# Two gated FFT-convolution layers and two MLPs, forward and backward, on one core: a reordered opening, other changes of order, and the product of the convolved k with v on GpSimd

## The chip, the cores and the metric

The kernel runs on one core of a Trainium2 chip. Its engines are named as in the profile: PE is TensorE (matrix products and transposes into PSUM), DVE is VectorE, ACT is ScalarE, POOL is GpSimd, and SP is the engine that issues most DMAs. Each engine runs its own instructions in a fixed order, and they wait for each other by semaphores. The time of a run is its device time in microseconds (us). All times below are in us unless they are marked ns.

## The reference, cut to what matters

```python
def _A_ref(q, k, v, shift_k, ssm_k, ssm_D):
    k_shift = sum over t < 4 of k_pad[:, t:t + S, :] * shift_k[:, 3 - t]
    kv = k_shift * v
    y = irfft(rfft(kv, 2 * S) * rfft(ssm_k, 2 * S))[:S]
    y = y + kv * ssm_D
    return q * y

def _B_ref(x, w1, w2):
    return silu(x @ w1) @ w2

x = A_q
x = x + _A_ref(layernorm(x), A_k, A_v, A_shift_k, A_ssm_k, A_ssm_D)
x = x + _B_ref(layernorm(x), B_w1, B_w2)
x = x + _A_ref(layernorm(x), A_k, A_v, A_shift_k, A_ssm_k, A_ssm_D)
x = x + _B_ref(layernorm(x), B_w1, B_w2)
```

S is 2048, the width D is 448 and the inner width F is 1792; the data are bf16. Both layers share their weights, and so the convolution result y is the same in both. What is computed is x and the gradients with respect to eight inputs, for a given grad_out: nine outputs.

## The kernel before

The work is done in three parts.

**The opening, `_ssm_prefix`,** makes y. The FFT of 4096 points is split in two stages, each of them matrix products on PE. `_fft_stage1` takes ssm_k over the long axis into A1K. `turn` (L348) transposes sixteen 128x128 blocks of it, group g of seven, into Z. `_fft_stage2` takes chunks of 1024 columns (14 of them, NCI) through the small DFT, and the function it is given gets the result from PSUM: `cons_ka` copies it to Ka (the memory of Z), stores every second chunk pair to DRAM (spec_K, L400), and for the later chunks issues the two DMAs of `_swap_halves_dma` (L244 and L245), which write KB, Ka with its halves swapped. On the side of the data, `conv(h, jq)` does the short convolution of k on PE for one of eight pieces (two column halves h, four row groups jq); ACT copies its result to ks (L372), POOL issues the store of ks to DRAM (KS_d, L374), and DVE multiplies ks by v to kvt (L376). `stage1_kv` takes kvt through stage 1 (L386) one loop step later, into A1kv; it is then turned into Zkv, and stage 2 over Zkv hands each chunk to `cons_prod`: a copy to Zf (the memory of A1K), a store (spec_KV, L443), and the products pa = Zf * Ka (L449) and pb = Zf * KB (L450) on DVE. Two chunks later `_fft_inv_stage2_chunk` takes pa and pb back (L226, L227), and the last stage (L475) makes Ysb, which is y. `_Bal` keeps a running sum of planned load for ACT and DVE, and gives each PSUM copy to the engine that has less; `_copy` shows as L111 on ACT and L113 on DVE.

In program order the opening runs: a loop over h = 0 and 1 and the four jq, which does conv, stage1_kv of the piece before, and then for h = 0 two turns of A1K, for h = 1 two chunks of K's stage 2; then the swaps of the first four chunk pairs, the last stage1_kv, K's remaining chunks 8 to 13, the LayerNorm of the first rows, all seven turns of A1kv, and stage 2 of kv with its products.

**`Main.run`** goes over four chunks c of 512 rows. `H(c, L)` (L is the layer) multiplies by w1: seven tiles fp of two blocks of 128 rows of F, each into a PSUM tile ps_h with two buffers (tag "mm", which ps_g shares). Of every tile ACT makes aT by silu (L614), and a copy of the tile goes to dT, on DVE where fp is in the argument dv and on ACT elsewhere. `slope` later replaces dT by silu's derivative on ACT (L626). `O` multiplies aT by w2 (L633) and adds to X. `G` makes the gradient behind w2 (ps_g, L652), whose PSUM copy ghT is multiplied by dT on DVE (L668 and L800). `N` multiplies by w1 (L683) and goes through the LayerNorm's backward `_ln_bwd`. `T` and `T2` are transposes on PE (L525, L723), copied by ACT to nT. `_ln` is a forward LayerNorm (bn_stats is L259, the power rstd on POOL L266, the normalised n L273), `fwd0` and `fwd1` are the two of them that stand ahead of a layer, with the gate by Y. PE's order is written out by `weave`, whose letters take one step from each generator; the order of DVE, ACT and POOL is chosen by the framework's scheduler when the kernel is built, within what `issue_after(x)` (put in behind x) and `keep_in_program_order` demand.

**`Jobs`** makes the weight gradients (L924): groups of four products (a unit), taken from a generator wherever PE is to have work of this kind. `bank` says which PSUM buffer a group sums in: "mm" has two, "tr" one, which the transposes use. **`_ssm_suffix`** takes the gradient back through the FFTs, with `jobs.run(n)` between its steps: a first stage (L206), `spectrum` (L1132, two parts u for each of seven pairs cp), the inverse (L1145), `ps_gkv` (L1189, eight steps i, copied by ACT to gkv, L1191), and the gradients of ssm_k and shift_k, for which four copies make skmask (L1218). What is left of the jobs runs at the end.

## Time and profile before

| what | us |
|---|---|
| runs of the kernel, median of 3 (lowest, highest) | 750.91 (748.93, 752.5) |
| the profiled execution, its own time | 744.07 |
| its span in the trace | 742.3 |
| granted clock, mean | 0.997 |

The busy time of the engines by stage of the profiled execution (the stages are cut by TensorE's instructions):

| from | to | stage | PE | DVE | ACT | POOL |
|---|---|---|---|---|---|---|
| 0 | 25.37 | loads, FFT stage 1 of ssm_k, transposes of k | 19.30 | 13.22 | 15.01 | 3.60 |
| 25.37 | 102.22 | the rest of the opening | 67.68 | 65.53 | 61.57 | 24.06 |
| 102.22 | 172.20 | first G, H(0,0), O, fwd1, G, H(0,1), O | 63.31 | 41.99 | 47.99 | 10.50 |
| 172.20 | 477.80 | the loop over the chunks | 300.22 | 198.95 | 216.23 | 23.69 |
| 477.80 | 519.66 | the last chunk's backward, with jobs | 40.63 | 18.52 | 10.24 | 2.71 |
| 519.66 | 691.00 | the backward FFTs, with jobs | 164.91 | 120.73 | 93.03 | 52.21 |
| 691.00 | 742.30 | the last gradients and jobs | 44.98 | 24.29 | 5.18 | 9.97 |

A stage's length less PE's busy time is what PE waited there: 9.2 in the opening's second row, 6.7 in the third, 5.4 in the long fourth. Rows of the timeline give the start, the duration, the engine, the line, and at the end in brackets how long the engine had been idle and what released it. Durations of neighbouring instructions overlap, since they are pipelined: the distance of two starts is what one costs.

### The profile page before, as it was taken

How to read it: one execution, taken by the hardware profiler on the slowest of the kernel's cores; microseconds unless marked ns; L12 is line 12 of the kernel's file. 1: busy time of each engine (PE TensorE's matmuls, PEld its weight loads, DVE VectorE, ACT ScalarE, POOL GpSimd, SP SyncE). 2: the span in 40 equal slices, each digit the busy share in tenths (PEclk: the TensorE clock that was granted, in tenths of full speed). 3: DMA queues.
4: the chain of work that ended last, by engine and by line, in shares of the span. 5: the costliest groups of instructions: out<-in, count | busy, mean ns of one | idle time of the engine just before them, and what ended most of it. 6: DMA issues, size and time to landing. Idle time of an engine off the chain costs nothing.

```text
span 742.3 us, 12705 instructions
## 1 busy us (share of the span) xinstructions
PE 701.0 (94%) x4947; PEld 395.2 (53%) x4976; DVE 483.2 (65%) x1140; ACT 449.3 (61%) x572; POOL 126.7 (17%) x212
## 2 busy tenths in 40 slices
PE   6998888989999999999999999999989999989996
PEld 4876644435444444444444544545466666657553
DVE  4789855856686747856379523925158769879760
ACT  4887966688866968669677794132755555455100
POOL 1134410210011100201001100000221234244130
PEclk9999999999999999999999999999999999999999
DMA  9949699799979999589875998189997898789870
GB/s 324 271 148 289 234 281 176 139 233 229 231 181 228 236 239 210 101 211 256 190 183 118 246 228 312 27 191 236 348 411 263 266 331 297 230 304 353 294 226 19
DMA packets 195485, 172.40 MB, mean 232 GB/s; under 512 B 142850, under 2 KB 173698, under 8 KB 194272
## 3 DMA queue, kind: packets, MB, share of 16 engines
q1 hardware_dynamic: 180896, 115.53, 61.7%
q0 software_dynamic: 14064, 56.04, 22.0%
q8 instruction: 39, 0.64, 0.4%
q14 instruction: 22, 0.18, 0.1%
q10 hardware_dynamic: 464, 0.00, 0.0%
HBM read 73.06 MB, written 60.10 MB: 179 GB/s over the span
## 4 chain that ended last, share of the span: by engine, by line
PE 41%; issue 21%; ACT 7%; DMA 7%; DVE 6%; POOL 3%; POOLq 0%; ACTq 0%; DVEq 0%
PE ps_d L924 11%; PE ps_h L611 9%; PE ps_n L683 6%; PE ps_o L633 5%; PE ps_g L652 3%; ACT dT L626 3%; DMA out_dram<-dout 2%; PE ps_v L227 2%; PE ps_v L226 2%; DMA go<-in_grad_out_dram 1%; DVE ln_st L259 1%; ACT aT L614 1%; POOL rstd L266 1%; DMA Minvs<-c_minv 1%; ACT dT L111 1%
## 5 line engine op out<-in xcount | busy, mean ns | idle before, releaser
L611 PE MATMUL ps_h<-nT,w1sb 112*128 112x512 bf16 x448 | 104.4, 379 | 6.9 <-ACT dT L111 2.9
L924 PEld LDWEIGHTS <-dstat 128*128 128x128 bf16 x800 | 75.7, 98 | 64.5 <-issue 0.6
L683 PE MATMUL ps_n<-w1T,ghT 128*128 128x448 bf16 x448 | 95.3, 353 | 1.3 <-DVE ghT L668 1.2
L633 PE MATMUL ps_o<-w2sb,aT 128*128 128x448 bf16 x448 | 88.5, 352 | 0.0
L652 PE MATMUL ps_g<-nT,w2T 128*128 128x512 bf16 x378 | 86.6, 379 | 0.7
L666 ACT CAST ghT<-ps_g 128x1024 bf16<-128x1024 f32 (+1 forms) x67 | 53.5, 821 | 53.0 <-PE ps_g L652 53.0
L614 ACT ACTIVATE aT<-ps_h 128x1024 bf16<-128x1024 f32 (+1 forms) x72 | 58.4, 834 | 34.9 <-PE ps_h L611 32.1
L611 PEld LDWEIGHTS <-w1sb 112*128 112x128 bf16 x448 | 43.8, 98 | 59.7 <-issue 10.2
L652 PEld LDWEIGHTS <-w2T 128*128 128x128 bf16 x448 | 43.7, 98 | 51.7 <-issue 0.7
L849 DVE SCALAR_TENSOR_TENSOR lb_v<-lb_u,n 128x448 bf16<-128x448 bf16 x48 | 29.9, 623 | 63.0 <-ACT lb_u L687 62.6
L683 PEld LDWEIGHTS <-ghT 128*128 128x128 bf16 x448 | 43.2, 98 | 43.9 <-DVE ghT L668 3.6
L633 PEld LDWEIGHTS <-aT 128*128 128x128 bf16 x448 | 43.5, 98 | 40.1
L626 ACT ACTIVATE dT<-dT 128x1024 bf16<-128x1024 bf16 (+1 forms) x64 | 54.6, 936 | 0.1
L266 POOL TENSOR_TENSOR rstd<-ln_ve,mhalf 128x2 f32<-128x2 f32 (+2 forms) x27 | 22.3, 827 | 178.2 <-DVE ln_ve L264 178.2
L924 PE MATMUL ps_d<-n3m,dstat 128*128 128x448 bf16 x224 | 48.2, 352 | 0.2
L924 PE MATMUL ps_d<-n1m,dstat 128*128 128x448 bf16 x224 | 48.1, 352 | 0.2
L111 ACT CAST dT<-ps_h 128x1024 bf16<-128x1024 f32 (+1 forms) x54 | 48.0, 906 | 0.0
L226 PE MATMUL ps_v<-Gsb,pa 128*128 128x128 bf16 x336 | 43.8, 222 | 2.7 <-DVE pa L449 2.6
L227 PE MATMUL ps_v<-Gsb,pb 128*128 128x128 bf16 x336 | 42.9, 222 | 2.4 <-DVE pb L450 1.9
L687 ACT ACTIVATE lb_u<-ps_n,rstd 128x448 bf16<-128x448 f32 x32 | 20.7, 646 | 31.8 <-PE ps_n L683 18.1
L924 PE MATMUL ps_d<-go,dstat 128*128 128x448 bf16 x176 | 37.2, 352 | 0.4 <-DMA go<-in_grad_out_dram 0.4
L226 PEld LDWEIGHTS <-pa 128*128 128x128 bf16 x336 | 33.3, 99 | 7.9 <-DVE pa L449 4.7
(208 smaller groups left out, 1193.0 us busy)
## 6 DMA issues: line engine op xcount, KB each, us to landing
dstat<-g_d SPq DMA_DIRECT2D x28, 512.0 KB, 6.0
dstat<-a_d SPq DMA_DIRECT2D x26, 512.0 KB, 5.8
a_d<-turned SPq DMA_DIRECT2D x16, 512.0 KB, 3.7
g_d<-turned SPq DMA_DIRECT2D x16, 512.0 KB, 3.5
a_d<-turned SPq DMA_DIRECT2D x16, 384.0 KB, 2.9
g_d<-turned SPq DMA_DIRECT2D x16, 384.0 KB, 2.9
N_d<-n POOLq DMA_DIRECT2D x10, 448.0 KB, 5.4
spec_K<-Z POOLq DMA_DIRECT2D x7, 512.0 KB, 6.6
```

The costliest lines, as they stand in the source:

```text
L111: nc.scalar.copy(out, in_)
L226: nc.tensor.matmul(pv[:, i, :], lhsT=pa[:, i * P:(i + 1) * P], rhs=k.Gsb[:, ga, :], start=True, stop=False)
L227: nc.tensor.matmul(pv[:, i, :], lhsT=pb[:, i * P:(i + 1) * P], rhs=k.Gsb[:, gb, :], start=False, stop=True)
L611: nc.tensor.matmul(ps[:, u, :], lhsT=self.w1sb[:, dc, ft * P:(ft + 1) * P], rhs=nT[:DC, dc, :], start=(dc == 0), stop=(dc == ND - 1))
L614: self.last_silu = nc.scalar.activation(aT[hh][:, o:o + hi - lo, :], ps[:, lo:hi, :], ACT.Silu)
L626: self.nc.scalar.activation(d[:, o:o + n, :], d[:, o:o + n, :], ACT.Derivative_silu)
L633: nc.tensor.matmul(po[:, :D], lhsT=aT[ft // 7][:, ft % 7, tl * P:(tl + 1) * P], rhs=self.w2sb[:, ft, :], start=(ft == 0), stop=(ft == NF - 1))
L652: nc.tensor.matmul(ps[:, u, :], lhsT=self.w2T[:, b, ft * P:(ft + 1) * P], rhs=gT[:, b, :], start=(b == 0), stop=(b == ND - 1))
L666: nc.scalar.copy(g, ps[:, lo:hi, :])
L683: nc.tensor.matmul(pn[:, :D], lhsT=gh[ft // 7][:, ft % 7, tl * P:(tl + 1) * P], rhs=self.w1T[:, ft, :], start=(ft == 0), stop=(ft == NF - 1))
L849: nc.vector.scalar_tensor_tensor(out=v[:], in0=u0, scalar=-1.0 / D, in1=n_t, op0=ALU.mult, op1=ALU.mult, accum_out=cp[:, 1:2])
L924: self.nc.tensor.matmul(ps[:, :D], lhsT=st[:, t, :], rhs=mov[:, t, :], start=(first and t == 0), stop=(last and t == NT - 1))
```

## The change

1. **`_ln` gets `behind`:** its bn_stats are put in behind a given DVE instruction. For `fwd0` of c >= 1 that is the last product dT * ghT of the last G (`self.g_last`), for `fwd1(c + 1)` the last instruction of `_ln_bwd` (`self.chain`, which `_ln_bwd` now returns).
2. **kvt** (ks times v, 128x896, eight times) is computed by POOL in place of DVE, and the balance counts nothing for it.
3. **stage1_kv** copies both halves of its PSUM tile in one instruction (16 in place of 32).
4. **The opening's order:** in the h = 1 half, K's stage 2 runs chunks 0-3, 4-7, 8-10 and 11-13, and three turns of A1kv (g = 0, then 1 and 2) are done there. The swaps of all seven pairs are issued behind the loop. Then come the last stage1_kv, chunks 0 to 5 of kv's stage 2, the LayerNorm, turns 3 to 6 with the products of chunks 0 to 5 between them, and chunks 6 to 13 with a product after each. The copy and store of a chunk (`cons_x`) are separated from its products (`prod`).
5. **x0c0 and gb0** are loaded by SP, behind the transposing load of w2T, and not by POOL.
6. **H:** where a tile's copy is on DVE, its silu and its copy are split in halves. H(0, 1) copies all seven tiles on DVE (before: tiles 3 and 5); the H of later chunks copy tile 5 on DVE where c is 0 or L is 1 (before: none).
7. **`slope(dT1)`** issues its last two small pieces behind the last copy of the transposes to nT (`self.last_copy`).
8. **Jobs and the suffix:** group 4 sums in the bank "tr", no longer in "mm"; two more units run in the first `spectrum`, and four more between the first four `ps_gkv` steps; skmask is copied by POOL.

```diff
@@ -249,14 +249,17 @@
-def _ln(k, pool, c, src, si, n_g, groups=((0, 4),), pin=False, eng=None):
+def _ln(k, pool, c, src, si, n_g, groups=((0, 4),), pin=False, eng=None, behind=None):
     nc = k.nc
...
         for tl in range(lo, hi):
-            i = nc.vector.bn_stats(out=st[:, tl, :], in_=src(tl))
+            with ExitStack() as es:
+                if behind is not None:
+                    es.enter_context(k.tc.issue_after(behind.ins))
+                i = nc.vector.bn_stats(out=st[:, tl, :], in_=src(tl))
             if pin:
@@ -321,7 +324,7 @@
         nc.sync.dma_start_transpose(out=k.w2T[:, 0:3, :], in_=k.B_w2[:, 0:384])
-        nc.sync.dma_start_transpose(out=k.w2T[:, 3:4, :], in_=k.B_w2[:, 320:448])
+        w2 = nc.sync.dma_start_transpose(out=k.w2T[:, 3:4, :], in_=k.B_w2[:, 320:448])
@@ -373,8 +376,7 @@
             kvt = work.tile([P, 4, DH], BF16, name="kvt", tag="pb", bufs=3)
-            nc.vector.tensor_tensor(out=kvt[:], in0=ks[:], in1=vn[:, 4 * jq:4 * jq + 4, ds], op=ALU.mult)
-            bal.add("dve", 0.62)
+            nc.gpsimd.tensor_tensor(out=kvt[:], in0=ks[:], in1=vn[:, 4 * jq:4 * jq + 4, ds], op=ALU.mult)
             return kvt
@@ -384,9 +386,8 @@
                         nc.tensor.matmul(ps[:, w, c, :DH], lhsT=k.M1sb[:, n2 + w, c, :], rhs=kvt[:, u + w, :], start=True, stop=True)
-                for w in range(2):
-                    _copy(nc, bal.pick(2 * DH), A1kv[:, 56 * h:56 * (h + 1), :, n2 + w, :].rearrange("p dh c ds -> p c dh ds"),
-                          ps[:, w, :, :DH].rearrange("p c (dh ds) -> p c dh ds", ds=4))
+                _copy(nc, bal.pick(4 * DH), A1kv[:, 56 * h:56 * (h + 1), :, n2:n2 + 2, :].rearrange("p dh c n ds -> p c dh n ds"),
+                      ps[:, :, :, :DH].rearrange("p n c (dh ds) -> p c dh n ds", ds=4))
@@ -395,10 +396,41 @@
                 lo, hi = (ci - 1) * 1024, (ci + 1) * 1024
-                if ci > 8:
-                    _swap_halves_dma(k, KB, Ka, lo, hi, nc.gpsimd)
                 nc.gpsimd.dma_start(out=k.SPEC_d["K"][:, lo:hi], in_=Ka[:, lo:hi])
+        B1 = A1kv[:].rearrange("p a c n s -> p a (c n s)")
+        Zf = A1K[:].rearrange("p a c n s -> p (a c n s)")
+
+        def cons_x(ci, ps):
+            sl = slice(ci * 1024, (ci + 1) * 1024)
+            _copy(nc, bal.pick(1024), Zf[:, sl], ps[:])
+            if ci % 2 == 1:
+                st = nc.gpsimd.dma_start(out=k.SPEC_d["KV"][:, (ci - 1) * 1024:(ci + 1) * 1024], in_=Zf[:, (ci - 1) * 1024:(ci + 1) * 1024])
+            if ci == 3:
+                with tc.issue_after(st.ins):
+                    nc.gpsimd.memset(k.w2T[0:64, 3, :], 0.0)
+
+        hold = []
+
+        def prod(ci):
+            sl = slice(ci * 1024, (ci + 1) * 1024)
+            pa = work.tile([P, 1024], BF16, name="pa", tag="pa", bufs=4)
+            pb = work.tile([P, 1024], BF16, name="pb", tag="pb", bufs=3)
+            nc.vector.tensor_tensor(out=pa[:], in0=Zf[:, sl], in1=Ka[:, sl], op=ALU.mult)
+            nc.vector.tensor_tensor(out=pb[:], in0=Zf[:, sl], in1=KB[:, sl], op=ALU.mult)
+            bal.add("dve", 1.4)
+            hold.append((pa, pb, ci))
+            if len(hold) > 2:
+                pa, pb, cj = hold.pop(0)
+                _fft_inv_stage2_chunk(k, pa, pb, False, B1, cj, psum)
+
+        k.x0c0 = _hd(k, [P, 4, D], "x0c0")
+        k.gb0 = _hd(k, [P, 4, D], "gb0")
+        with tc.issue_after(w2.ins):
+            nc.sync.dma_start(out=k.x0c0[:], in_=_pm(k.A_q[0])[:, 0:4, :])
+            nc.sync.dma_start(out=k.gb0[:], in_=_pm(k.grad_out[0])[:, 0:4, :])
+
+        spans = ((0, 4), (4, 8), (8, 11), (11, 14))
         prev = None
@@ -411,50 +443,28 @@
                 else:
-                    _fft_stage2(k, Z, psum, cons_ka, range(2 * i, 2 * i + 2))
-        for i in range(4):
+                    _fft_stage2(k, Z, psum, cons_ka, range(*spans[i]))
+                    for g in ((), (), (0,), (1, 2))[i]:
+                        turn(B1, Zkv, g)
+        for i in range(7):
             _swap_halves_dma(k, KB, Ka, 2048 * i, 2048 * (i + 1), nc.gpsimd)
         stage1_kv(*prev)
-        _fft_stage2(k, Z, psum, cons_ka, range(8, NCI))
+        _fft_stage2(k, Zkv, psum, cons_x, range(6))
...
         nc.sync.dma_start(out=k.w1sb[:], in_=k.B_w1.rearrange("(c p) f -> p c f", p=DC))
-        k.gb0 = _hd(k, [P, 4, D], "gb0")
-        nc.gpsimd.dma_start(out=k.gb0[:], in_=_pm(k.grad_out[0])[:, 0:4, :])
-        k.x0c0 = _hd(k, [P, 4, D], "x0c0")
-        nc.gpsimd.dma_start(out=k.x0c0[:], in_=_pm(k.A_q[0])[:, 0:4, :])
         k.na0 = _hd(k, [P, 4, D], "na0")
...
-        B1 = A1kv[:].rearrange("p a c n s -> p a (c n s)")
-        Zf = A1K[:].rearrange("p a c n s -> p (a c n s)")
-
-        A1f = A1kv[:].rearrange("p a c n s -> p a (c n s)")
-        for g in range(7):
-            turn(A1f, Zkv, g)
-        hold = []
-
-        def cons_prod(ci, ps):
...
-        _fft_stage2(k, Zkv, psum, cons_prod)
+        for g in range(3, 7):
+            turn(B1, Zkv, g)
+            if g < 6:
+                prod(2 * (g - 3))
+                prod(2 * (g - 3) + 1)
+        for ci in range(6, NCI):
+            _fft_stage2(k, Zkv, psum, cons_x, (ci,))
+            prod(ci)
@@ -586,15 +596,15 @@
             src = lambda tl: xc[:, tl, :]
-            self.a_fwd(c, 0, src, n00, ((0, 4),))
+            self.a_fwd(c, 0, src, n00, ((0, 4),), self.g_last)
         n01 = self.t([P, 4, D], "n01", bufs=2)
...
-    def fwd1(self, c):
+    def fwd1(self, c, behind=None):
         n10, n11 = self.t([P, 4, D], "n10"), self.t([P, 4, D], "n11")
         pairs = ((0, 2), (2, 4)) if c else ((0, 2), (2, 3), (3, 4))
-        self.a_fwd(c, 2, self.xs(c), n10, pairs)
+        self.a_fwd(c, 2, self.xs(c), n10, pairs, behind)
         _ln(self.k, self.ch, c, self.xs(c), 3, n11, pairs)
@@ -609,18 +619,18 @@
                     nc.tensor.matmul(ps[:, u, :], lhsT=self.w1sb[:, dc, ft * P:(ft + 1) * P], rhs=nT[:DC, dc, :], start=(dc == 0), stop=(dc == ND - 1))
-            for lo, hi in self.parts(fp):
+            for lo, hi in ((0, 1), (1, 2)) if fp in dv else self.parts(fp):
                 hh, o = divmod(2 * fp + lo, 7)
                 self.last_silu = nc.scalar.activation(aT[hh][:, o:o + hi - lo, :], ps[:, lo:hi, :], ACT.Silu)
-            for lo, hi in ((0, 2),) if fp < 6 else ((0, 1), (1, 2)):
+            for lo, hi in ((0, 2),) if fp < 6 and fp not in dv else ((0, 1), (1, 2)):
                 _copy(nc, nc.vector if fp in dv else nc.scalar, self.dpart(dT, 2 * fp + lo, 2 * fp + hi), ps[:, lo:hi, :])
...
     def slope(self, dT, behind=None):
-        with self.tc.issue_after((behind or self.last_silu).ins):
-            for d in dT:
+        for i, d in enumerate(dT):
+            with self.tc.issue_after((behind if behind is not None and i > 2 else self.last_silu).ins):
                 n = min(2, d.shape[1])
@@ -665,7 +675,7 @@
                 if dT is not None:
-                    nc.vector.tensor_tensor(out=g, in0=d, in1=g, op=ALU.mult)
+                    self.g_last = nc.vector.tensor_tensor(out=g, in0=d, in1=g, op=ALU.mult)
             yield
@@ -690,7 +700,7 @@
                 nc.vector.scalar_tensor_tensor(out=u1[:], in0=Gt, scalar=k.rstd[2][:, t:t + 1], in1=self.Y[:, t, :], op0=ALU.mult, op1=ALU.mult, accum_out=cp[:, 4 + tl, 0:1])
-                _ln_bwd(k, self.ch, u1[:], n_a[:, tl, :], cp[:, 4 + tl, :], Gt, Gt)
+                self.chain = _ln_bwd(k, self.ch, u1[:], n_a[:, tl, :], cp[:, 4 + tl, :], Gt, Gt)
             else:
@@ -771,7 +782,7 @@
         r = []
-        weave("H" * 7, H=self.H(0, 1, nT, r, (3, 5)))
+        weave("H" * 7, H=self.H(0, 1, nT, r, range(7)))
         for c in range(4):
@@ -810,13 +821,13 @@
                 if c == 0:
-                    weave("NTNTNHNHNHNHNHHHH", N=n, T=self.T(self.n0[1][1], nT, NBLK), H=self.H(c + 1, 0, nT, r))
+                    weave("NTNTNHNHNHNHNHHHH", N=n, T=self.T(self.n0[1][1], nT, NBLK), H=self.H(c + 1, 0, nT, r, (5,)))
                 else:
...
                 weave("OOOOOOTOTO", O=self.O(c + 1, 0, aT), T=tg)
-                self.fwd1(c + 1)
+                self.fwd1(c + 1, self.chain)
                 g = self.G(gT, gh1, dT0)
@@ -824,7 +835,7 @@
                     weave("G" * 7, G=g)
-                self.slope(dT1)
+                self.slope(dT1, self.last_copy)
             else:
@@ -837,7 +848,7 @@
                 nT = self.nT()
-                weave("NNTNTNHNHNHNHNHHH", N=n, T=self.T(self.n1[1], nT, NBLK), H=self.H(c + 1, 1, nT, r))
+                weave("NNTNTNHNHNHNHNHHH", N=n, T=self.T(self.n1[1], nT, NBLK), H=self.H(c + 1, 1, nT, r, (5,)))
             else:
@@ -851,7 +862,7 @@
     nc.vector.tensor_tensor(out=v[:], in0=v[:], in1=u0, op=ALU.add)
-    nc.vector.tensor_tensor(out=G_out, in0=v[:], in1=g_res, op=ALU.add)
+    return nc.vector.tensor_tensor(out=G_out, in0=v[:], in1=g_res, op=ALU.add)
@@ -928,7 +939,7 @@
             self.n_bank += 1
-        bufs = {"po": 2, "jb": 1, "mm": 2}[tag]
+        bufs = {"po": 2, "jb": 1, "mm": 2, "tr": 1}[tag]
         if tag == "mm":
@@ -971,7 +982,7 @@
         yield from self.group((3,), keys, (go, g2), self.fin_w2, tags=("jb",))
-        yield from self.group((4,), keys, (go, g2), self.fin_w2, tags=("mm",))
+        yield from self.group((4,), keys, (go, g2), self.fin_w2, tags=("tr",))
         yield from self.group((5, 6), keys, (go, g2), self.fin_w2)
@@ -1131,7 +1142,7 @@
                     nc.scalar.copy(Zf[cp][:, u * 1024:(u + 1) * 1024], ps[:])
-                    jobs.run(1)
+                    jobs.run(1 if cp else 2)
                 _swap_halves(k, xsw, Zf[cp])
@@ -1192,7 +1203,7 @@
             nc.vector.tensor_tensor(out=gks[:, sl, :], in0=gkv, in1=gks[:, sl, :], op=ALU.mult)
-            jobs.run(1)
+            jobs.run(2 if i < 4 else 1)
         for lo, hi in ((0, 112), (112, 127)):
@@ -1215,7 +1226,7 @@
         for b in range(0, P, 32):
-            nc.vector.tensor_copy(mask[b:b + 32, :], k.ident[b:b + 32, b:b + 32])
+            nc.gpsimd.tensor_copy(mask[b:b + 32, :], k.ident[b:b + 32, b:b + 32])
         pd = psum.tile([P, 2, 512], FP32, name="ps_sk", **mm)
```

More of the change, by code (lines that the diff above doesn't have):

```diff
@@ L431, in _ssm_prefix @@
-        Zf = A1K[:].rearrange("p a c n s -> p (a c n s)")
-        A1f = A1kv[:].rearrange("p a c n s -> p a (c n s)")
-        for g in range(7):
-            turn(A1f, Zkv, g)
-        hold = []
-        def cons_prod(ci, ps):
-            sl = slice(ci * 1024, (ci + 1) * 1024)
-            xs = Zf[:, sl]
-            _copy(nc, bal.pick(1024), xs, ps[:])
-            if ci % 2 == 1:
-                st = nc.gpsimd.dma_start(out=k.SPEC_d["KV"][:, (ci - 1) * 1024:(ci + 1) * 1024], in_=Zf[:, (ci - 1) * 1024:(ci + 1) * 1024])
-            if ci == 3:
-                with tc.issue_after(st.ins):
-                    nc.gpsimd.memset(k.w2T[0:64, 3, :], 0.0)
-            pa = work.tile([P, 1024], BF16, name="pa", tag="pa", bufs=4)
-            pb = work.tile([P, 1024], BF16, name="pb", tag="pb", bufs=3)
-            nc.vector.tensor_tensor(out=pa[:], in0=xs, in1=Ka[:, sl], op=ALU.mult)
-            nc.vector.tensor_tensor(out=pb[:], in0=xs, in1=KB[:, sl], op=ALU.mult)
-            bal.add("dve", 1.4)
-            hold.append((pa, pb, ci))
-            if len(hold) > 2:
-                pa, pb, cj = hold.pop(0)
-                _fft_inv_stage2_chunk(k, pa, pb, False, B1, cj, psum)
@@ L547, in parts, with a_fwd @@
         return [(0, 2)] if fp not in (3, 6) else [(0, 1), (1, 2)]
-    def a_fwd(self, c, si, src, n_g, groups):
+    def a_fwd(self, c, si, src, n_g, groups, behind=None):
         nc, X = self.nc, self.X
@@ L556, in a_fwd @@
             return
-        _ln(self.k, self.ch, c, src, si, n_g, groups)
+        _ln(self.k, self.ch, c, src, si, n_g, groups, behind=behind)
         self.gate(c, src, n_g)
@@ L729, in run @@
         self.n0, self.gyt = {}, {}
+        self.g_last = None
         jobs = k.jobs = Jobs(k, self)
```

## The prediction

> **What bounds the kernel now.** I read the page first, its head, its engine shares and its slices.
>
> ```profile
> span 742.3 us, 12705 instructions
> PE 701.0 (94%) x4947; PEld 395.2 (53%) x4976; DVE 483.2 (65%) x1140; ACT 449.3 (61%) x572; POOL 126.7 (17%) x212
> PE   6998888989999999999999999999989999989996
> DVE  4789855856686747856379523925158769879760
> ```
>
> TensorE (PE) works 94% of the span. Its thin places are the slices up to about 150 us and a few single slices. The timeline shows TensorE's last product at about 736 and VectorE's (DVE) last instruction at 716.8: TensorE sets the end, so a TensorE gap that closes is time won, and one that opens is time lost. The second view, busy time by stage, shows the opening:
>
> ```profile
> 25.37:40.00 14.63, 14.63 (x263) 14.62 (x262) 10.36 (x15) 11.55 (x12) 2.29 (x3) 1.00 0.92 172
> 40.00:54.30 14.30, 13.92 (x182) 11.06 (x181) 12.13 (x18) 10.86 (x18) 5.06 (x8) 1.00 0.43 143
> 65.00:75.00 10.00, 7.37 (x71) 5.23 (x71) 8.87 (x15) 7.04 (x7) 4.50 (x10) 0.83 1.03 283
> 85.00:95.00 10.00, 7.13 (x100) 5.62 (x100) 9.43 (x16) 7.86 (x8) 4.71 (x7) 1.00 0.48 162
> ```
>
> Columns after the length are TensorE, its weight loads, VectorE, ScalarE (ACT), GpSimd (POOL), the granted clock, the DMA share and GB/s. Up to 54.3 TensorE is full and VectorE and ScalarE have room (22.5 and 22.4 of 28.9 us); later VectorE is full (9.43 of 10) and TensorE waits. Third, TensorE's waits over the whole run:
>
> ```profile
> PE ps_h L611 <- ACT dT L111: 2.9, 6, 1.6
> PE ps_t L525 <- ACT nT L526: 2.5, 6, 0.5
> PE ps_gkv L1189 <- ACT gkv L1191: 1.9, 1, 1.9
> PE ps_s L206 <- ACT A1g L111: 1.7, 6, 0.5
> PE ps_s L1132 <- ACT Zw L1133: 1.6, 1, 1.6
> PE ps_n L683 <- DVE ghT L668: 1.2, 2, 0.6
> ```
>
> Each row gives the total, the number of waits and the longest. They are small, so every edit of the loops and the suffix is worth tenths of a microsecond to some three.
>
> **The opening: the product kvt on GpSimd.** The rows are GpSimd's before, and VectorE's product.
>
> ```profile
> 2.06 0.32 POOL masks.py:199 TENSOR_SCALAR_AFFINE_SELECT ident<-ident 128x128 bf16<-128x128 bf16 x1
> 28.35 0.78 POOL L374 DMA_DIRECT2D KS_d<-ks  x1 [17.52 <-ACT ks L372]
> 40.37 0.75 POOL L374 DMA_DIRECT2D KS_d<-ks  x1 [3.58 <-ACT ks L372]
> 53.65 0.62 DVE L376 TENSOR_TENSOR kvt<-ks,v_n 128x896 bf16<-128x896 bf16 x1
> ```
>
> Before, kvt follows ks on VectorE in 0.62. After, GpSimd first issues KS_d (0.75) and then multiplies; no row shows such a product there. From below: its MEMSET of 128x1344 takes 1.24, by elements 0.83 for 896, with nothing read. From above: the select takes 0.32 for 128 columns, so 7 x 0.32 = 2.24 for 896, and twice that, 4.5, if a second input costs a full pass. (GpSimd's two-input rstd rows, 792 ns for 2 columns and 1065 for 4, are powers, and I leave them out.) I take 2.0, a little under the select's 2.24, since its 0.32 holds a fixed part.
>
> The first four products in stage1_kv (L386) start at 30.31, 34.45, 38.58 and 41.81, with no TensorE gap ahead. KS_d leaves GpSimd at 29.13, 32.66, 36.78 and 41.12. With 2.0 on top kvt is ready at 31.13, 34.66, 38.78 and 43.12. The first is 0.8 late. That covers the second, whose conv already stood ahead of the first stage1_kv; the third is 0.2 late beyond the common shift, the fourth 1.3. Sum +2.3. In the second half (h=1) the KS_d rows are 3.4 to 3.65 apart, GpSimd needs 0.75 + 2.0 + 0.55 (the spec_K store) = 3.3, and the step gets longer there; I add nothing. At 0.83 the stall is 0.1. At 4.5 GpSimd's step of 5.25 is over TensorE's 4.13 and the lag grows to about 10, h=1 included. What waits on GpSimd behind these: spec_K and the swaps, 14 issues of 0.52. The swaps now all come after the loop, about 61 to 69 instead of from 54.65 on; the first pb, before at 69.58, needs only the first pair. The load of w1sb, whose buffer is freed later, is wanted at 110.
>
> [...]
>
> **The opening: the new order.** Six chunks of K's stage 2 (copies of 1.01 on ScalarE or 1.22 on VectorE, say 6 x 1.1) and three turns (1.21 or 1.87, say 3 x 1.5) move from the crowded stretch after 54 into the loop, where 13 us of the two engines lie idle, and two products leave VectorE (2 x 0.54). That is 12.2, or 6.1 for each of two engines. TensorE's part of it (6 x 0.43 + 3 x 0.9 = 5.3) comes into a stretch where TensorE is full. Net -0.8. One merged copy of stage1_kv (896 columns, 1.02) in place of two (0.54 to 0.62 each): 0.15 x 8 after mid-loop over two engines, -0.5. So -1.3, and with the stall +1.0. From below: TensorE works 32.9 of the 40.7 us from 54.3 to 95, so at most 7.8 can go, and I count -6 as the floor of the whole opening; +9 is its ceiling. x0c0 and gb0 on the queue of SP land by about 45 by the order there, and are used from 60.8 on: nothing.
>
> **H(0,0) and H(0,1).** These rows are TensorE's and VectorE's around H(0,1):
>
> ```profile
> 149.42 3.62 PE L611 MATMUL ps_h<-nT,w1sb 112*128 112x512 bf16 x16
> 154.65 3.72 PE L611 MATMUL ps_h<-nT,w1sb 112*128 112x512 bf16 x16 [1.61 <-ACT dT L111]
> 160.81 3.61 PE L611 MATMUL ps_h<-nT,w1sb 112*128 112x512 bf16 x16 [0.36 <-DVE dT L113]
> 164.26 7.92 PE L633 MATMUL ps_o<-w2sb,aT 128*128 128x448 bf16 x41
> ...
> 156.78 1.31 DVE L273 TENSOR_SCALAR n<-X,rstd,ln_nmr 128x448 bf16<-128x448 bf16 x4
> 159.53 1.23 DVE L113 CAST dT<-ps_h 128x1024 bf16<-128x1024 f32 x1 [1.43 <-ACT aT L614]
> ```
>
> Halves in H(0,0): in the built program the first copy half waits for both silu halves, as it did before for the last tile (silus to 125.91, copy at 125.95). Nothing overlaps; halves cost 1.09 + 1.29 where wholes cost 1.02 + 1.23, 0.13 in each of three cycles: +0.4. H(0,1) is where I expect the loss. Its seven tiles have two PSUM buffers. Before, ScalarE freed them (first wait 1.61); VectorE's own two copies came after all of fwd0(1), whose last n ends at 158.09. The built order still puts all of fwd0(1) ahead of the copies, and now all seven are VectorE's. So tile 2 starts at 158.09 + 1.29 = 159.4, not 154.65. From there H(0,0) shows the pace of two buffers emptied by silu and then VectorE: 4.26 for two tiles (114.39, 118.65, 122.91), plus the 0.13. Tile 6 starts at 159.4 + 2 x 4.3 = 168.0 and O 1.7 later, at 169.7 instead of 164.26. The slopes and ghT behind it shift with O. +5.3. Bounds: +3.5 (TensorE's own 1.73 a tile once started) to +6.5.
>
> **The loops.** Four kinds of gaps: ghT at 226.60 and 318.04, behind bn_stats of x0c that now come after (0.57 + 0.58); nT at 209.53, 300.97 and 397.58, behind slopes of which the last two now follow the copy (3 x 0.51); and 0.29 twice where one more copy is VectorE's. -3.3: nothing covers these gaps, so each counts in full. What is late next is LN's n and the two slopes with what is queued behind them on VectorE and ScalarE, by about 1 us, and TensorE wants these only a stage later. Bounds -3.3 to -0.6.
>
> **The suffix.** Six job units of 4 products (0.76 each) come earlier. The two in the spectrum fill 0.76 of the 1.60 at 556.72 and the 0.48 at 559.79; three before 661.48 are 2.3 against its 1.90, which ends behind a load (the gks data) and not behind TensorE. The same products are missing at the tail. The sums of job group 4 no longer hold one of the two buffers that the first backward stage (L206) needs from 519.66 on: its six waits of 1.7 in all go, since a second buffer lets TensorE run on while ScalarE copies. -3.1 - 1.7 = -4.8, bounds -4.8 to -1.5. skmask's copies (1.88 together) leave VectorE, which has 20 us of slack, and go to an idle GpSimd: nothing.
>
> **Sum.** +1.0 + 0.4 + 5.3 - 3.3 - 4.8 = -1.4 on the profiled execution of 744.07 (its span 742.3 and 1.8 around it). That execution lies 6.8 under the median of the runs, 750.91, so I add the difference to the median: 749.5.
>
> **Rivals.** *First, faster:* the opening gains more. TensorE waits there for pa, pb and A1K one after another, and with K's spectrum and three turns done ahead, the products start as soon as a chunk is there. If 5 of the 7.8 us go and kvt takes about 1.1 (stall 0.3), the opening is 0.3 - 5 = -4.7 and the sum -4.7 + 0.4 + 5.3 - 8.1 = -7.1: 743.8. For it speaks that nothing but order stands ahead of the first pb; against it VectorE's 9.43 of 10. *Second, slower:* the small gains of loops and suffix don't come, because another wait of nearly the same length stands behind each: with -0.6 and -1.5 in place of -8.1 the sum is +4.6, 755.5. That is the change not doing what it says. For it: each gap has several inputs, and a wait is put down to the last only. Against: in the ghT gap VectorE's rows show plain bn_stats in front. *Third, slower:* GpSimd's product sets TensorE's pace in the loop (over 3.4 us each, since 0.75 + 3.4 = 4.13), and the time goes over 754.7 from a stall of 7.5, at about 4.0 us each. At 4.5 the sum is +6.3: 757.2. For: two inputs, no row; against: the select's 2.24.
>
> **Chances.** A run of this kernel tells about 0.5% (3.75 us) from no change: faster is under 747.2, slower over 754.7. Forecast 0.39, first rival 0.31, second 0.18, third 0.12. So faster 0.31, same 0.39, slower 0.30. The range goes from 743.5 (the first rival) to 757 (the second and most of the third); the forecast's own is 747.3 to 753, from H(0,1)'s bounds and half of the opening's.
>
> **What will show it.** kvt on GpSimd at 2.0 and gaps of 0.8 and 1.3 ahead of L386's products; H(0,1)'s third tile about 10 us after its first, with a wait on VectorE's dT of some 6; no gap over 0.3 for ghT and nT in the loops; the waits at Zw under 0.9, at gkv and L206 near nothing. I'm wrong if H(0,1) keeps its 15 us, or if the opening up to the first ps_g (102.22 before) moves by more than 3.

## The result and the profile after

The changed kernel takes 756.61 us (median of 6 runs, 755.28 to 757.63), the kernel before 749.21 (6 runs, 744.01 to 752.5). The ratio on record is 1.0125, with a 95% interval of 1.0089 to 1.0162, and the two medians alone give 1.0099: the change makes the kernel slower, by some 7.4 us by the medians and 9.4 by the ratio. 749.5 was predicted, within 743.5 to 757.0, with the most likely case "no change". The time lies at the range's upper end, and the sign of the forecast was wrong.

The page of the changed kernel, its head, its engine shares and the slices of TensorE and VectorE:

```profile
span 755.1 us, 12746 instructions
PE 699.7 (93%) x4946; PEld 396.3 (52%) x4976; DVE 490.1 (65%) x1148; ACT 438.0 (58%) x566; POOL 145.0 (19%) x222
PE   5996887969999999999999999999999999999995
DVE  3677874776678656877368743824258769859750
```

TensorE's work is what it was (699.7 against 701.0); what grew is its idle time and the time at a lower clock. The granted clock is 0.986 over the span, before 0.997. GpSimd's busy time grew by 18.3 us, most of it the eight products.

Some of TensorE's waits after the change (total, number, longest):

```profile
PE ps_h L621 <- DVE dT L113: 9.2, 5, 6.3
PE ps_kt L336 <- DMA KB<-in_A_ssm_k_dram: 6.0, 2, 5.6
PE ps_v L227 <- DVE pb L420: 5.5, 4, 3.5
PE ps_d L935 <- DMA dstat<-a_d: 2.9, 2, 1.8
...
PE ps_s L388 <- POOL kvt L379: 1.4, 2, 0.7
...
PE ps_gkv L1200 <- ACT gkv L1202: 0.9, 1, 0.9
```

Before, the three that stand first here were:

```profile
PE ps_kt L333 <- DMA KB<-in_A_ssm_k_dram: 4.5, 1, 4.5
...
PE ps_h L611 <- DVE dT L113: 2.3, 4, 0.7
...
PE ps_v L227 <- DVE pb L450: 1.9, 4, 1.2
```

Two rows have grown most: the copies dT on VectorE, now with one wait of 6.3, and the product pb. The product on GpSimd itself, the change's headline, has a row of 1.4. The row at ps_kt is a load of the input ahead of the first conv. The waits for ghT, and those of the suffix at L206 for A1g, are gone from the list, as the prediction had it.

Setting the starts of the same TensorE work in the two traces side by side gives where the time goes. The columns are before, after, and the difference:

| first instruction of | before | after | after - before |
|---|---|---|---|
| the first conv | 25.37 | 27.05 | +1.68 |
| the first G | 102.22 | 108.50 | +6.28 |
| O of (0,0) | 124.63 | 131.71 | +7.08 |
| H(0,1) | 149.42 | 156.50 | +7.08 |
| O of (0,1) | 164.26 | 178.65 | +14.39 |
| the last chunk's last N | 506.04 | 517.05 | +11.01 |
| the last job | 733.05 | 742.70 | +9.65 |
| end of the span | 742.3 | 755.1 | +12.8 |

So the opening from the first conv on costs 4.6, H(0,0) 0.8 with the G before it, H(0,1) 7.3; the loops win 3.4 and the suffix 1.4. From the last job's start to the end of the span it takes 12.4 where it took 9.25: another 3.1, and an experiment below narrows down where they come from. These make +11.0. The 1.7 ahead of the first conv are waits for loads of the input, which vary (the first conv starts at 23.7 to 27.4 in the executions below). The rest is a matter of the executions that were profiled: that of before (744.07) lies 5.1 under its median, that of the changed kernel (756.85) 0.2 over its own, so 12.8 in the spans are 7.4 in the medians.

### The profile page after: what moved, and what is told of

It reads as the page before. It is cut to its first block, busy times and chain, and to the rows that moved or that the text cites. A ratio compares the mean times of both kernels' runs of the same rounds, so it can differ in the third digit from the quotient of the medians.

```text
span 755.1 us, 12746 instructions
## 1 busy us (share of the span) xinstructions
PE 699.7 (93%) x4946; PEld 396.3 (52%) x4976; DVE 490.1 (65%) x1148; ACT 438.0 (58%) x566; POOL 145.0 (19%) x222
## 4 chain that ended last, share of the span: by engine, by line
PE 53%; issue 13%; DMA 11%; DVE 11%; ACT 5%; POOL 5%; SPq 0%; POOLq 0%; ACTq 0%; DVEq 0%
PE ps_n L693 11%; PE ps_g L662 11%; PE ps_h L621 10%; PE ps_o L643 9%; PE ps_d L935 3%; PE ps_d L972 2%; DMA dstat<-a_d 2%; DMA gks<-gks 1%; DMA spec_KV<-A1K 1%; DMA K_sb<-in_A_ssm_k_dram 1%; DMA ksf<-KS_d 1%; PE ps_t L535 1%; PE ps_s L206 1%; DVE ln_st L262 1%; DVE dT L113 1%
## 5 line engine op out<-in xcount | busy, mean ns | idle before, releaser
L621 PE MATMUL ps_h<-nT,w1sb 112*128 112x512 bf16 x448 | 106.9, 386 | 12.1 <-DVE dT L113 9.2
L624 ACT ACTIVATE aT<-ps_h 128x512 bf16<-128x512 f32 (+1 forms) x86 | 59.2, 727 | 47.0 <-PE ps_h L621 46.8
L935 PE MATMUL ps_d<-go,dstat 128*128 128x448 bf16 x176 | 37.6, 353 | 2.9 <-DMA dstat<-a_d 1.8
L227 PEld LDWEIGHTS <-pb 128*128 128x128 bf16 x336 | 33.3, 99 | 11.2 <-DVE pb L420 7.2
L111 ACT CAST dT<-ps_h 128x1024 bf16<-128x1024 f32 (+1 forms) x44 | 38.8, 900 | 0.0
L935 PE MATMUL ps_d<-X,dstat 128*128 128x448 bf16 x176 | 37.2, 353 | 1.0 <-DMA dstat<-a_d 1.0
```

The lines of the kernel that those rows point to most:

```text
L111: nc.scalar.copy(out, in_)
L227: nc.tensor.matmul(pv[:, i, :], lhsT=pb[:, i * P:(i + 1) * P], rhs=k.Gsb[:, gb, :], start=False, stop=True)
L621: nc.tensor.matmul(ps[:, u, :], lhsT=self.w1sb[:, dc, ft * P:(ft + 1) * P], rhs=nT[:DC, dc, :], start=(dc == 0), stop=(dc == ND - 1))
L624: self.last_silu = nc.scalar.activation(aT[hh][:, o:o + hi - lo, :], ps[:, lo:hi, :], ACT.Silu)
L935: self.nc.tensor.matmul(ps[:, :D], lhsT=st[:, t, :], rhs=mov[:, t, :], start=(first and t == 0), stop=(last and t == NT - 1))
```

## The experiments

Each ran on the chip beside the kernel before. Differences of times to the changed kernel are between runs of several sets, and the kernel before has medians of 744.17 to 749.21 in them, so such a difference can be off by 5 us. The ratio to the kernel before of the same set is given too, and it is what the experiments are compared by; the changed kernel's is 1.0125.

**kvt back on VectorE, in the changed kernel.**

```diff
-            nc.gpsimd.tensor_tensor(out=kvt[:], in0=ks[:], ...)
+            nc.vector.tensor_tensor(out=kvt[:], in0=ks[:], ...)
+            bal.add("dve", 0.62)
```

> The changed kernel with one edit undone: kvt is multiplied on VectorE again. Theory A (the product on GpSimd costs the opening): its stalls of 0.65 and 0.73 at L388 go, the last pair product is not 1.89 in front of the second swap DMA of the first pair, so that KB comes about 2 us earlier; the first ps_g starts about 3 us earlier after the first conv, and the run takes some 753 to 754. Rival B (the moved K chunks and turns delay the last conv, and with it the swaps, whoever multiplies): the gaps ahead of the first pb stay near 5 us in all, and the run stays within 1.5 us of the changed kernel's 756.6.

756.65 us (ratio 1.0134, 1.0077 to 1.0192): no gain, rival B by the time. In its trace the stalls at L388 are gone, the first pair's second swap is issued 36.1 after the first conv, no longer 37.6 (61.42 - 25.37 against 64.67 - 27.05), and the second product starts 1.7 earlier, counted the same way. But from the first conv to the first ps_y it takes 75.38, exactly as with GpSimd (102.43 - 27.05). And then ps_y itself is slow. Its timeline, and the busy time of two stages of 3.4 us (TensorE, weight loads, VectorE, ScalarE, GpSimd, granted clock, DMA share, GB/s):

```profile
100.75 9.14 PE L486 MATMUL ps_y<-A1kv,Minvsb 128*128 128x448 bf16 x32 [1.10 <-ACT A1kv L111]
```

```profile
96.80:100.20 3.40, 1.24 (x16) 0.99 (x17) 1.78 (x3) 0.51 (x1) 0.45 (x1) 0.95 0.98 386
100.20:103.60 3.40, 2.85 (x8) 1.12 (x8) 1.12 (x2) 0.50 (x1) 0.00 (x0) 0.50 1.03 379
```

ps_y takes 9.14 where it takes 6.23 in all the other executions but one (7.90): behind a stretch in which TensorE worked only 1.24 of 3.4, its granted clock is 0.50 over the next one. The product's engine is not what makes this opening slow.

**The product on GpSimd alone, in the kernel before.**

> The kernel before with one edit: kvt is multiplied by GpSimd. Theory A (the product by itself costs its stalls and what it puts in front of the swaps): stalls of about 0.7 and 0.7 at the first half's products and 1 to 2 at the swaps, so the run takes 2 to 4 us more than the kernel before. Rival B (VectorE's relief pays for the stalls): within 1 us of the kernel before.

748.26 us (ratio 1.0045, 1.0003 to 1.0088), theory A: the first G is 2.4 us later, and 2.8 later counted from the first conv. Two of its eight starts of stage1_kv's products, with GpSimd around the last:

```profile
30.66 0.93 PE L385 MATMUL ps_s<-kvt,M1sb 128*128 128x224 bf16 x8 [0.60 <-POOL kvt L376]
58.56 0.93 PE L385 MATMUL ps_s<-kvt,M1sb 128*128 128x224 bf16 x8 [2.38 <-POOL kvt L376]
```

```profile
56.63 1.89 POOL L376 TENSOR_TENSOR kvt<-ks,v_n 128x896 bf16<-128x896 bf16 x1
58.45 0.59 POOL L399 DMA_DIRECT2D spec_K<-Z  x1
59.04 0.56 POOL L244 DMA_DIRECT2D KB<-Z  x1
```

There are four stalls, 0.60, 0.73, 0.70 and 2.38, 4.4 in all, of which 2.8 are left at the first G. That VectorE's relief pays the rest back was not tested. The product takes 1.89 to 1.90 in every instance.

**The changed opening alone, in the kernel before** (the whole `_ssm_prefix` of the changed kernel, with kvt on GpSimd).

> The kernel before with the changed opening alone (its new order, kvt on GpSimd, merged copies, loads on SP). Theory A (the opening as a whole loses, by the late KB and the lower clock behind the wait): first conv to first ps_g 81 to 82 in place of 76.85, and the run takes 4 to 5 us more than the kernel before. Rival B (the opening's loss in the profile of the changed kernel is one execution's): under 2 us more.

756.99 us (ratio 1.0122, 1.0048 to 1.0195), theory A. First conv to first ps_g: 108.15 - 26.69 = 81.46, against 81.45 in the changed kernel and 76.85 before. The opening alone costs 4.6 in the trace. That it repeats to a hundredth is luck: the three executions below that keep this order, the product on GpSimd and the swaps and w1sb in their places (H(0,1) as before, the suffix as before, the two loads on GpSimd) have 82.40, 82.11 and 81.58. In the time there is some more, about 9 us by the ratio; 3.2 of it stand at the program's end, which takes 12.37 here as in the changed kernel, and the interval covers the rest.

**The swaps on SP's queue, in the changed kernel.**

```diff
-            _swap_halves_dma(k, KB, Ka, 2048 * i, 2048 * (i + 1), nc.gpsimd)
+            _swap_halves_dma(k, KB, Ka, 2048 * i, 2048 * (i + 1), nc.sync)
```

> The changed kernel with the fourteen swap DMAs issued by SP in place of GpSimd, so that they queue behind no product and no spec_K store (the load of w1sb, on the same queue, comes after them). Theory A (the first pb waits for KB, which is late by GpSimd's queue): KB's first pair is issued as soon as the last conv has read KB, at about 60, the gaps of 1.96 and 3.54 ahead of the first products go for the most part, and the opening gets 4 to 6 us shorter: 751 to 753. Rival B (the DMA engines are full then, and the landing of 10 us is what makes KB late): the issue moves, the landing does not by more than 1.5, and the run stays over 755.

749.92 us (ratio 1.0056, 1.0022 to 1.0091), theory A by the time: 6.7 less than the changed kernel by the medians, some 5.2 by the ratios. Here is what it removes. The changed kernel's GpSimd, SP and VectorE, from the last product on:

```profile
59.85 0.55 POOL L244 DMA_DIRECT2D KB<-Z  x1 [0.48 <-PE ps_cv L373]
60.91 0.79 POOL L377 DMA_DIRECT2D KS_d<-ks  x1 [0.51 <-ACT ks L375]
61.73 1.89 POOL L379 TENSOR_TENSOR kvt<-ks,v_n 128x896 bf16<-128x896 bf16 x1
63.56 1.12 POOL L399 DMA_DIRECT2D spec_K<-Z  x2
63.65 0.34 SPq L455 DMA_DIRECT2D w1sb<-in_B_w_dram  x1
64.67 0.52 POOL L245 DMA_DIRECT2D KB<-Z  x1
...
74.89 0.69 DVE L420 TENSOR_TENSOR pb<-A1K,KB 128x1024 bf16<-128x1024 bf16 x1 [2.47 <-issue]
```

Its TensorE at the first two products:

```profile
71.88 0.23 PE L226 MATMUL ps_v<-Gsb,pa 128*128 128x128 bf16 x1 [1.96 <-DVE pa L419]
75.64 0.29 PE L227 MATMUL ps_v<-Gsb,pb 128*128 128x128 bf16 x1 [3.54 <-DVE pb L420]
```

And the same with the swaps on SP:

```profile
70.02 0.23 PE L226 MATMUL ps_v<-Gsb,pa 128*128 128x128 bf16 x1 [1.96 <-DVE pa L419]
71.22 0.29 PE L227 MATMUL ps_v<-Gsb,pb 128*128 128x128 bf16 x1 [0.96 <-DVE pb L420]
```

In the changed kernel the pair's first half is released by the last conv (59.85) and lands 3.9 later. The second half stands behind a store, a product and two more stores; it lands 10.1 after its issue, at 74.81, and pb starts at 74.89. The wait row names VectorE; the cause is a DMA two steps back. On SP's queue the first pair is issued at 52.52 and 53.11, ahead of the last conv (55.95), so it doesn't need that conv, and its halves land 4.4 and 6.5 after their issues. From the first conv to the first ps_g it is now 77.54, and 5.77 of absolute time are won at the first G, of which 1.86 are the loads of that execution.

This run moves a second thing, though. The load of w1sb, whose buffer is free when the last product has read v (its wait on SP is put down to that product), leaves SP at 63.65 in the changed kernel, 1 us ahead of the late half. Here it queues behind the swaps and leaves at 79.00. The run can't tell the swaps' queue from the load's time; the next one can.

**w1sb behind the swaps, in the changed kernel.** The load is issued by GpSimd behind the last swap, at 79.37; the swaps stay on GpSimd.

> The changed kernel with the load of w1sb (1.6 MB) issued by GpSimd behind the last swap, in place of SP at 63.65. Theory A (the load takes the DMA engines from the swaps, whose first pair needs 10 us to land): KB's first pair lands 3 to 5 us earlier, the gap of 3.54 ahead of the second product goes, and the run takes 752 to 754. Rival B (the swaps are late by their place in GpSimd's queue alone): the gap stays over 2, and the run over 755.

The second half of the pair, and the second product:

```profile
64.63 0.52 POOL L245 DMA_DIRECT2D KB<-Z  x1
```

```profile
73.04 0.29 PE L227 MATMUL ps_v<-Gsb,pb 128*128 128x128 bf16 x1 [0.96 <-DVE pb L420]
```

The half is issued as late as in the changed kernel, behind the same product and stores, and lands after 4.9 in place of 10.1. The gap ahead of the second product shrinks from 3.54 to 0.96, as with the swaps on SP, and from the first conv to the first ps_g it takes 77.41, 4.0 less than in the changed kernel. So the load of w1sb beside the pair is enough for the whole loss, and theory A holds for the opening; the place in GpSimd's queue alone brings no such gap. The time (774.61; 766.21 to 781.96) doesn't show the gain, since three spec_KV stores are issued at 102.67 only, behind a store for which GpSimd had waited 15.99, and ScalarE then stands idle for 27.25. For the whole run this is inconclusive.

**H(0,1) with two copies on VectorE again.**

```diff
-        weave("H" * 7, H=self.H(0, 1, nT, r, range(7)))
+        weave("H" * 7, H=self.H(0, 1, nT, r, (3, 5)))
```

> The changed kernel with one edit undone: H(0,1) copies only its tiles 3 and 5 on VectorE. Theory A (VectorE reaches the seven copies only after fwd0(1), which costs 6.3 of wait and, behind the wait, a granted clock of 0.79): from the start of H(0,1) to the start of O it takes about 15, not 22.15, and the run about 749.5. Rival B (the wait only moves to ScalarE's copies and its slopes behind O): H(0,1) gets shorter by 7 but the stages up to the next H give back more than 3, and the run takes over 753.

749.42 us (ratio 1.0056, 1.0026 to 1.0086), theory A: H(0,1) takes 14.91, and 7.2 are won. The loop gives nothing back: the starts stay 9.0 ahead through it (1.8 of it from earlier). At the last job 7.4 are left, since this execution waits 3.63 at L1236 in the suffix. By the ratios some 5.2 are won in all. The changed kernel's TensorE and VectorE at H(0,1):

```profile
156.50 3.62 PE L621 MATMUL ps_h<-nT,w1sb 112*128 112x512 bf16 x16
166.41 8.00 PE L621 MATMUL ps_h<-nT,w1sb 112*128 112x512 bf16 x24 [6.30 <-DVE dT L113]
174.96 3.85 PE L621 MATMUL ps_h<-nT,w1sb 112*128 112x512 bf16 x16 [0.55 <-DVE dT L113]
...
163.85 1.31 DVE L276 TENSOR_SCALAR n<-X,rstd,ln_nmr 128x448 bf16<-128x448 bf16 x4
165.08 2.47 DVE L113 CAST dT<-ps_h 128x512 bf16<-128x512 f32 x4
```

VectorE is through with fwd0(1) at 165.08 and only then makes the first copy. The 24 products behind the wait take 8.00; 24 x 0.216, the pitch elsewhere at full clock (1.73 for eight), is 5.2. The stages there (same columns as above) say why:

```profile
168.00:169.50 1.50, 1.50 (x5) 0.58 (x4) 0.00 (x0) 0.00 (x0) 0.00 (x0) 0.50 0.00 0
...
172.50:174.00 1.50, 1.49 (x7) 0.70 (x8) 0.39 (x1) 1.08 (x2) 0.00 (x0) 1.00 0.00 0
```

The granted clock is 0.50 from the end of the wait to 171.34, and the products start 0.43 apart there, 0.216 at 1.00.

**Both mends together.**

> The changed kernel with both mends: H(0,1) copies tiles 3 and 5 alone on VectorE, and the swap DMAs are issued by SP. If the two losses are separate, as their places 80 us apart say, the gains of 7.2 and 6.7 add: 742.5 to 743.5, that is as fast as the kernel before or 1 to 2 us faster. If they overlap (a common wait behind both), the run stays over 746.

745.08 us (ratio 0.9965, 0.9932 to 0.9999). By the medians that is 11.5 from the changed kernel, where the two give 13.9 singly; by the ratios it is 1.6%, some 12, where they give 0.7% each. In the traces the opening wins 3.9 (77.55 from the first conv to the first ps_g) and H(0,1) 7.2, 11.1 together. So the two add. The time lies between the 742.5 to 743.5 and the 746 that were expected for the two cases.

**Only the opening's order left.** kvt on VectorE, swaps on SP, H(0,0) and H(0,1) as before; the loops and the suffix are the changed ones.

> The changed kernel with kvt on VectorE, the swaps issued by SP, and H(0,0) and H(0,1) as before, so that only the opening's order differs in the opening. Theory A (the order itself is worth nothing, since VectorE and ScalarE have the same work and the last conv, which frees KB, comes later): first conv to first ps_g 76 to 78, as before (76.85), and a time of 742 to 745. Rival B (without the late KB the order wins the 3 to 6 us that TensorE idles there): first conv to first ps_g under 74, and under 740.

743.86 us (ratio 0.9960, 0.9933 to 0.9988), theory A: first conv to first ps_g 77.83, where the old order has 76.85 in the kernel before and 75.67 to 77.29 in the other four executions that have it with the product on VectorE. In the loop up to the last conv it takes 3.9 more, behind it 2.9 less. With everything that spoils it taken out (w1sb leaves behind the swaps here too), the new order is, in this one execution, 0.5 to 2.2 us worse than the old one.

**The loops alone, in the kernel before.**

> The kernel before with the loops' edits alone (bn_stats behind the last ghT product or the LayerNorm's backward, two small slopes behind the last copy, tile 5 copied on VectorE; tiles whole as before). Theory A (the prediction's loop term, which the two traces show as -3.4): from the start of the first H of the loop (ps_h 3) to the last one 3.3 us less, and the run takes 3 to 3.5 less than the kernel before. Rival B (the gain needs the shifted start of the changed kernel, since another wait is as long): under 1 us less.

740.92 us (ratio 0.9931, 0.9889 to 0.9973), theory A by the trace: it starts the loop 0.16 later than the kernel before and ends it 3.29 earlier, 3.45 won. The time gives some 5, and its interval covers the 3.45.

**The suffix's edits undone, in the changed kernel** (skmask stays on GpSimd).

> The changed kernel with the suffix's edits undone: job group 4 sums in the bank of ps_h and ps_g again, and no job unit is moved. Theory A (the 1.7 at L206 and the gaps filled by job units are given back as waits for the loads of dstat, 1.84 + 1.02, and at L1236): those waits go, the six waits at L206 return, and the run stays within 1.5 us of the changed kernel's 756.6. Rival B (the suffix's edits win the 3 to 5 us that the prediction gave them, and something else lost them): the run takes 3 us more, about 760.

764.1 us (ratio 1.0193, 1.0114 to 1.0272), rival B: 7.5 us slower than the changed kernel by the medians and some 5 by the ratios, whose intervals overlap. Three of the four runs take 763.8 to 765.3, one 755.67. The profiled one shows TensorE and VectorE:

```profile
678.25 1.65 PE L1200 MATMUL ps_gkv<-B1v,Minvs 128*128 128x448 bf16 x4 [6.46 <-ACT gkv L1202]
...
676.58 1.70 DVE L1205 TENSOR_TENSOR gks<-gkv,gks 128x896 bf16<-128x896 bf16 x3 [7.20 <-DMA gks<-in_A_v_dram]
```

The load of v into gks ends late in this execution, and TensorE has run out of work. From the last chunk's last N to the last job it takes 219.2, 7.0 more than in the changed kernel. In the kernel before the same wait was 1.90, in the loops alone 2.29, in the changed opening alone 1.59: it varies with the execution. The moved job units stand just there. That the other two long runs have the same wait isn't shown, since only one was profiled.

**Loops and suffix, in the kernel before,** with the opening and H as before; and the same with job group 4 in its old bank.

> The kernel before with the changed loops and the changed suffix, and the opening and H(0,1) as before. Theory A (the suffix's edits keep TensorE busy while gkv waits for its load, a wait that one execution shows as 1.6 and another as 6.46): no gap at L1200 over 1, the times of the runs lie closer together than the kernel before's 742 to 757, and the median is 737 to 739, under the 740.9 of the loops alone. Rival B (what the suffix wins is given back as waits for dstat and at L1236): 740 to 741.5, with waits for dstat of over 2 in the trace.

> The same, but job group 4 sums in the bank of ps_h and ps_g as before, so that of the suffix's edits the six moved job units and skmask are left. Theory A (the second buffer at L206 wins 1.7 that the waits for the dstat loads take back): the six waits at L206 are there, the two for dstat are not, and the time is within 1 us of the run with the bank moved. Rival B (the bank is worth its 1.7): 1.5 to 2 us slower than that run.

The times are 739.51 (ratio 0.9888, 0.9850 to 0.9926; 6 runs, 737.45 to 740.28) and 740.92 (ratio 0.9901, 0.9867 to 0.9935; 8 runs, 737.52 to 742.94). The first has the lowest median of all, about 1.1% under the kernel before, and no wait at gkv is left in its trace. The gain over the loops alone (740.92, 739.21 to 747.67) is small in the median, and for the first one theory A and rival B both hold in part: it also has waits of 1.6 for dstat and 2.1 at L1229. The bank is worth 1.4 by the medians, within the spread, so between the two theories it stays open.

**The two loads, each way.** One thing is left: with the old opening it takes 9.2 from the last job's start to the end in all five executions so far, with the changed one 11.9 to 12.4 in eight of nine, and the trace shows no other work there. The ninth, with w1sb late, has 9.15, so the first expectation below is wrong in saying that every execution with the changed opening has the long end. The first run moves the loads of x0c0 and gb0 to SP in the kernel before, the second moves them back to GpSimd in the changed one.

```diff
-        nc.gpsimd.dma_start(out=k.gb0[:], in_=...)
-        nc.gpsimd.dma_start(out=k.x0c0[:], in_=...)
...
+        with tc.issue_after(w2.ins):
+            nc.sync.dma_start(out=k.x0c0[:], in_=...)
+            nc.sync.dma_start(out=k.gb0[:], in_=...)
```

> The kernel before with x0c0 and gb0 loaded by SP behind w2T, as in the changed kernel, and nothing else. From the start of the last 16 products to the end of the span it takes 9.2 in every execution with the old opening and 11.8 to 12.4 in every one with the changed opening. Theory A (the end depends on how many DMAs GpSimd issued: two fewer with the loads on SP): 11.8 to 12.4 here. Rival B (another part of the opening): 9.2.

> The changed kernel with x0c0 and gb0 loaded by GpSimd at their old place. Theory A (the number of GpSimd's DMAs): from the last 16 products' start to the end of the span 9.2, and about 3 us less than the changed kernel's 756.6 unless the loads' place costs the opening. Rival B: 11.8 to 12.4 as in the changed kernel.

Theory A in both: 12.41 (751.7 - 739.29) in the first, 9.23 (751.5 - 742.27) in the second. The last store in the changed kernel, and with the loads on GpSimd again:

```profile
746.79 0.54 POOL L1024 DMA_DIRECT2D out_dram<-dout  x1 [5.51 <-ACT dout L1022]
```

```profile
748.27 0.54 POOL L1023 DMA_DIRECT2D out_dram<-dout  x1 [7.42 <-issue]
```

In the second GpSimd issues its last store 1.9 later after its last wait ("issue": nothing in the trace holds it), and still the program ends 3.2 earlier. That moving the two loads moves the end is shown in both kernels; why is not. They aren't needed for it: with w1sb on GpSimd the end is short although both loads are on SP. What goes with it in all sixteen traces is how many DMAs GpSimd issues, 173 or 172 with the 9.2, 171 or 157 with 11.9 to 12.4; SP's number goes the other way (239 and 240, 241 and 255), and the runs don't tell the two apart. One execution each (753.47 and 753.26) says little of the whole time; the first of them has the wait at gkv at 4.89. The swaps on SP take away fourteen more of GpSimd's DMAs and the end is 11.9, so it isn't a price for each DMA.

## Why the prediction was wrong, step by step

- **kvt on GpSimd, 2.0 us, stalls +2.3.** The duration was right: 1.89. The stalls in the first half are 0.65 and 0.73 where 0.8 and 1.3 were predicted, 1.4 in all, and the third rival is refuted. In the kernel before the same product gives 4.4 of stalls, so their size depends on the order around it.
- **"What waits on GpSimd behind these": this step failed.** The prediction let the swaps start at 61 and called it harmless, since "the first pb needs only the first pair", and asked of the load of w1sb only when it is wanted. It left out how long the pair takes to land, and what goes out beside it. The pair's second half, issued at 64.67 behind a product and three stores, lands after 10.1, because the 1.6 MB of w1sb leave 1 us ahead of it; with the load moved it lands after 4.9, from the same place in the queue, and the 4.0 us are gone. The trace of before already had such a landing, 10.5 beside w1sb, but ended it at 67.58, ahead of the first pb at 69.6. Product, stores and the longer loop (the last conv comes 5.2 later, 57.81 - 27.05 against 50.89 - 25.37) are what shifts both issues. This put 3.54 of wait ahead of the second product, and with it a granted clock of 0.50 until 79.18, 6.8 us of it in place of the 3.4 that the kernel before has at its first products. The opening moved by more than 3, one of the prediction's own signs of being wrong.
- **The new order, -1.3.** Wrong in sign: +1.0 against the kernel before, in one execution each, with the late swaps and GpSimd's product removed. The work moved into the loop made the loop longer by more (3.9) than the later part got shorter (2.9).
- **x0c0 and gb0 on SP, "nothing".** Their landing did no harm (first conv to first ps_g is 81.45 with them on SP and 81.58 with them on GpSimd), but the program's end comes 3.1 later. This term was missing, and its cause stays open.
- **H(0,0), +0.4.** 0.43 from H(0,0) to O.
- **H(0,1), +5.3.** The mechanism was right: tile 2 starts 9.91 behind tile 0, with a wait of 6.30 on the copies. The term was mis-sized by 2.0, and all of it lies behind tile 2, where 12.2 to O were measured and 10.3 predicted: the clock behind the wait, 0.50 up to 171.34, was left out. It measured 7.3.
- **The loops, -3.3.** -3.4 in the changed kernel, -3.45 alone. The waits for ghT went, nT's went from 0.51 to 0.30, and O got two new ones of 0.7 for X.
- **The suffix, -4.8.** -1.4 in the traces. The waits at L206 and Zw went, gkv's was halved (0.94), but jobs that run earlier need their loads earlier: dstat 1.84 and 1.02, go 1.04, and 0.96 at L1236. What the prediction didn't see is its worth as an insurance: 7.0 in the traced execution of the changed kernel without it, in which gks comes late.

With the measured terms the sum is 4.6 + 0.8 + 7.3 - 3.4 - 1.4 + 3.1 = +11.0 on the profiled execution, where -1.4 was predicted. Of the 12.4 between them the opening has 3.6 (4.6 in place of 1.0; the late KB alone is 4.0, and the rest of it came to 0.6), the program's end 3.1, the suffix 3.4 and H(0,1)'s clock 2.0; H(0,0) and the loops make up the rest. Adding a sum made on one short execution to the median then hid that the kernel before itself loses time in its other executions, most likely at gkv, where the changed one is insured, though that was not tested: the medians differ by 7.4 only. So it is in part luck that 756.61 still lies within the range. Of the rivals, the second (small gains don't come) holds for the suffix's traces only, and the first (the opening gains) is refuted.

## What to carry to other kernels

A product moved to an idle engine cost 1.4 of stalls in one order and 4.4 in another; ask also what that engine issues next, which loads its result sets free, and how long these DMAs take to land beside each other (here 10.1 beside w1sb, 4.9 without it). A copy put on another engine is as late as everything that the built order puts ahead of it there (here it came at 165.08, behind all of fwd0(1)), and the products behind a wait on TensorE are to be looked at too: behind the 6.30 here 24 of them took 8.00, not 5.2. When a DMA changes its queue, look at the program's last microseconds (9.2 or 12.4 here). A reorder that fills an engine in one stage with work from another must show idle time in the first stage on the engine that bounds it, here TensorE, and not on its helpers (here the loop took 3.9 more, what stands behind it 2.9 less).

## What the runs showed that was not expected

**The clock behind a wait.** The granted clock was 0.50 for 4.9 us behind the wait of 6.30 at H(0,1), for 3.5 behind the two waits of 1.96 and 3.54 in the opening, and for the 3.4 from 100.20 on at ps_y in one experiment, where the wait at ps_y was only 1.10 but TensorE had worked 1.24 of the 3.4 before. With the products 0.43 apart in place of 0.216, half of the 4.9 us are lost, 2.4, an estimate that fits the 2.0 by which H(0,1) exceeded its term. Apart from the one at the end, the trace of the kernel before has one stretch at 0.50, of 3.41 from 69.20 on, and the changed kernel's has two, of 6.83 each, from 72.36 and from 164.51 on. In the 3.41 ahead of these three TensorE had worked 1.30, 1.20 and 0.00. What sets the clock was not shown.

**A wait that comes and goes.** The kernel before ranges from 741 to 758 over the sets of runs here; with the loops and suffix changed it ranges over 2.8, in six runs. At gkv, behind the load of gks, the six traces with the old suffix show a wait between 1.6 and 6.5 (1.59, 1.90, 1.93, 2.29, 4.89, 6.46), the ten with the moved jobs none over 0.98. That it makes the whole spread was not tested.
